# Fourier transform over row pairs t and 448-t, and attention-times-v and Fourier products in parts per step

## The chip, the cores and the metric

The kernel runs on one core of a Trainium2 chip. The metric is the device time of one execution in microseconds (us), as the median of several runs; lower is better. The engines are TensorE (PE, matrix products, with PEld for its weight loads), VectorE (DVE), ScalarE (ACT), GpSimd (POOL) and SyncE (SP, which here only issues DMAs). Each works through its own queue of instructions in order. Products go to PSUM, in tiles of one bank, and DVE or ACT take them out; POOL works on SBUF alone.

## The reference

```
scores = scale * q @ k^T                      # (8, 12, 448, 448), head size 64
scores = einsum('bhij,hg->bgij', scores, w_pre)
attn   = softmax(scores)                      # over j, +1e-9 in the denominator
attn   = einsum('bhij,hg->bgij', attn, w_post)
x      = attn @ v                             # to (8, 448, 768)
X      = fft(fft(x, axis=1), axis=2)
u      = x + real(X)
un     = layernorm(u)
out    = u + relu(un @ w_ch1) @ w_ch2         # 768 -> 3072 -> 768
```

All data are float32, the two feed-forward weights arrive as float64.

## The kernel before

The kernel has two halves. `mix_phase` computes attention, mixing and the Fourier transform and writes u to a tensor in HBM, `u_scr`; `ffn_phase` normalizes u and runs the feed-forward part on blocks of 512 rows. The change is in the first half.

**Steps.** A step handles 5 x 12 score rows on 128 partitions, twice; three steps are a block of 56 rows, six a group of 112, 24 a batch (four groups), 192 in all. `s` counts steps, and step s works ahead: it starts the premix of step s+2. In each step PE makes the premix (L294, w_pre over the heads), DVE the negative row maximum (L301), ACT the exponential and its sum (L310). POOL adds 1e-9 to the sum (L318), DVE takes the reciprocal (L320), POOL scales the two halves of the tile (L323). Two steps later PE makes the postmix (L333, w_post) and DVE turns its result by 32 x 32 blocks into `Pv` (L344). Premix and postmix have one PSUM buffer each (`pmx`, `ppo`), everything else on PE shares four (`pms`).

**Fill work** is put between these by due times. The table at L512 gives each item a step, "tile" items stand between premix and postmix, "full" items behind the postmix, "none" items are DMAs. PE and DVE run in exactly the order in which the loop (L558) writes the instructions; ACT, POOL and SP are ordered by a scheduler. The fill items are:

- transpositions of q and k (L245) and scores q k^T (L268) into `Sb`, which SP's DMAs gather into `Kr` (L284), two steps ahead of the premix;
- `emit_av` (L350): attention times v for a group, 84 matmuls of 120 columns at once; ACT or DVE copy the result to `XT` (L381);
- `emit_x` (L387): `XT` is transposed to `X`, 112 rows by 768, and POOL folds the columns d and 768-d into an even part `xe` and an odd part `xo` (L403 to L406). The transform of a real row needs the cosine table on `xe` and the sine table on `xo` alone;
- `emit_z` (L412): the transform along the rows, one of seven column chunks at a time, from the four groups (four matmuls, L417) to `z`; frequencies 0 to 224 are computed, the others are mirrored copies;
- `emit_s2` (L429): the transform along the columns for one group, four matmuls from the even chunks and three from the odd (L437); DVE adds both to `X` (L445, L448), SP stores `X` to `u_scr` (L452);
- on DVE, four operations per step of the conversion of the weights from float64 (L472 to L483); in the steps listed in `sums` one.

A batch's `emit_z` and `emit_s2` come after its 24 steps, and so fall beside the next batch's steps; those of the last batch come after the last step. `ev.pick` hands copies out of PSUM to ACT or DVE by a running count of their costs; nearly all go to ACT.

## Time and profile before

| what | before |
|---|---|
| median of 3 runs | 2830.31 us (2822.34 to 2838.7) |
| profiled execution | 2837.51 us |
| its span, first to last instruction | 2835.6 us |
| busy: PE, DVE, ACT, POOL | 91%, 44%, 26%, 23% |
| first row maximum (L301) to the last | 42.5 to 1177.2 us |
| first product of the feed-forward half (L746) | 1242.35 us |

How to read it: the shares of busy time are averages over two very different halves. From about 1242 us on PE works nearly without a break; up to there it does not, and the work is spread over four engines. Where the prediction quotes windows, a row gives a stretch in us from the span's start, its length, and for each engine the busy time and in brackets the instructions, then the granted clock of PE, the share of the DMA engines and the rate in GB/s. A row of a group gives line, engine, operation, output <- input, shapes and count, then busy time, the mean of one in ns, and the idle time ahead of it with what ended it.

### The profile page before, as it was taken

Reading aid. Unit: us, or ns where it says so; the run is one execution under the profiler, and the core shown is the slowest. Engines: PE = TensorE matmul, PEld = TensorE weight load, DVE = VectorE, ACT = ScalarE, POOL = GpSimd, SP = SyncE. Lnnn points to the kernel's source line nnn. Section 1 sums busy time; section 2 is a strip of 40 time slices with the busy share of each in tenths; the row PEclk is TensorE's granted clock in tenths of the full one; section 3 lists DMA queues with packets and bytes.
Section 4 is the critical chain, followed back from the end, with each engine's and each line's share of the span. In section 5 each row is a group of like instructions: output and inputs, shape, how many; then the busy total and the mean of one; then the engine's idle time right before and its main releaser. Section 6 shows DMA issues by size and latency. Waiting matters only on the chain.

```text
span 2835.6 us, 47087 instructions
## 1 busy us (share of the span) xinstructions
...
## 2 busy tenths in 40 slices
...
GB/s 206 175 187 131 184 131 193 131 179 134 184 130 181 134 164 135 256 299 176 156 161 156 161 158 154 167 150 168 164 147 174 141 165 183 134 161 156 156 103 106
DMA packets 185110, 463.00 MB, mean 163 GB/s; under 512 B 22990, under 2 KB 128974, under 8 KB 172350
## 3 DMA queue, kind: packets, MB, share of 16 engines
...
HBM read 317.56 MB, written 59.77 MB: 133 GB/s over the span
## 4 chain that ended last, share of the span: by engine, by line
PE 61%; issue 12%; DVE 11%; DMA 9%; ACT 3%; POOL 2%; SPq 1%; ACTq 0%; POOLq 0%; DVEq 0%
PE psP L746 10%; PE psP L786 10%; PE psR L786 7%; PE psR L746 6%; PE ms L437 5%; PE ms L361 4%; PE mx L294 4%; PE psQ L786 3%; DVE nmx L301 3%; PE ms L268 3%; PE po L333 3%; DMA w1t<-w1f 3%; PE ms L417 3%; PE psQ L746 2%; DVE Pv L344 2%
## 5 line engine op out<-in xcount | busy, mean ns | idle before, releaser
L746 PE MATMUL psP<-ub,w1t 128*128 128x256 f32 x2016 | 473.0, 388 | 24.7 <-DVE mv L705 16.6
L746 PEld LDWEIGHTS psP<-ub,w1t 128*128 128x128 f32 x2016 | 388.7, 194 | 93.4 <-DMA w1t<-w1f 20.2
L786 PE MATMUL psP<-w2t,h 128*128 128x384 f32 x1344 | 436.9, 486 | 0.0
L786 PEld LDWEIGHTS psP<-w2t,h 128*128 128x128 f32 x1344 | 254.4, 190 | 173.4
L294 PE MATMUL mx<-Kr,kw 60*64 60x448 f32 x1536 | 203.6, 584 | 143.8 <-ACT PP L310 137.6
L310 ACT ACTIVATE PP<-mx,nmx 128x448 f32<-128x448 f32 x384 | 240.2, 630 | 359.4 <-DVE nmx L301 348.0
L323 POOL TENSOR_SCALAR PP<-PP,rcp 128x448 f32<-128x448 f32 x384 | 252.6, 667 | 218.8 <-DVE rcp L320 151.6
L723 POOL TENSOR_TENSOR ub<-ub 128x768 f32<-128x768 f32 x28 | 51.0, 1842 | 1060.9 <-ACT ub L718 1060.3
L344 DVE STREAM_TRANSPOSE Pv<-po 128x896 f32<-128x896 f32 x192 | 212.9, 1109 | 148.6 <-PE po L333 147.7
L301 DVE TENSOR_REDUCE nmx<-mx 128x2 f32<-128x896 f32 x192 | 207.1, 1079 | 104.3 <-PE mx L294 102.4
L746 PE MATMUL psR<-ub,w1t 128*128 128x256 f32 x1008 | 231.7, 379 | 0.0
L786 PE MATMUL psR<-w2t,h 128*128 128x384 f32 x672 | 220.0, 486 | 0.0
L117 ACT COPY Sb<-ms 124x448 f32<-124x448 f32 x379 | 186.1, 541 | 96.5 <-PE ms L268 80.6
L746 PEld LDWEIGHTS psR<-ub,w1t 128*128 128x128 f32 x1008 | 191.2, 190 | 26.9 <-DMA w1t<-w1s 0.9
L333 PE MATMUL po<-PP,kw 60*32 60x448 f32 x3072 | 199.5, 573 | 7.5 <-DVE rcp L320 4.4
L268 PE MATMUL ms<-kT,qT 64*64 64x448 f32 (+1 forms) x1536 | 205.5, 575 | 0.0
L294 PEld LDWEIGHTS mx<-Kr,kw 60*64 60x64 f32 x1536 | 42.9, 134 | 247.8 <-ACT PP L310 198.9
L795 DVE TENSOR_TENSOR u<-u,psP 128x384 f32<-128x384 f32 x56 | 31.1, 555 | 341.6 <-PE psP L786 341.6
L786 PEld LDWEIGHTS psR<-w2t,h 128*128 128x128 f32 x672 | 126.3, 190 | 84.3
L361 PEld LDWEIGHTS ms<-Pv,vv 64*64 64x64 f32 x5376 | 154.6, 138 | 23.5 <-issue 18.4
L361 PE MATMUL ms<-Pv,vv 64*64 64x120 f32 x5376 | 158.1, 272 | 8.0 <-issue 6.2
L718 ACT COPY ub<-psQ 128x384 f32<-128x384 f32 x56 | 24.9, 481 | 497.0 <-PE psQ L716 497.0
...
## 6 DMA issues: line engine op xcount, KB each, us to landing
Kr<-Sb SPq DMA_DIRECT2D x768, 105.0 KB
...
raw<-in_moe_w_ch_dram POOLq DMA_DIRECT2D x96, 384.0 KB, 4.6
w1t<-w1f SPq DMA_DIRECT2D x84, 384.0 KB
...
```

The costliest lines, as they stand in the source:

```text
L117: self.nc.scalar.copy(out=out, in_=in_)
L268: nc.tensor.matmul(pss[x][64 * y:64 * y + r0 + 64 - lo, :S], st["qT", xx][64 * x:64 * x + 64, y, lo:r0 + 64], st["kT", xx][64 * x:64 * x + ...
L294: nc.tensor.matmul(mx[64 * z:64 * z + 64, x, :S], kw1[64 * x:64 * x + KR, :], Kr[64 * x:64 * x + KR, z, :], start=True, stop=True)
L301: nc.vector.tensor_reduce(nmx[:, :], steps[T]["mx"][:, :, :S], axis=AX.X, op=ALU.max, negate=True)
L310: nc.scalar.activation(PP[:, x, :], steps[T]["mx"][:, x, :S], ACTF.Exp, bias=steps[T]["nmx"][:, x:x + 1], accum_out=den[:, x:x + 1])
L323: nc.gpsimd.tensor_scalar(PP[:, x, :], PP[:, x, :], rcp[:, x:x + 1], 1.0, op0=ALU.mult, op1=ALU.mult)
L333: nc.tensor.matmul(po[o:o + 32, z, :S], kw2[64 * z:64 * z + KR, y, :], PP[64 * z:64 * z + KR, :, c * HS:(c + 1) * HS], start=True, stop=True)
L344: nc.vector.transpose(g["Pv"][:, T % GT, :].rearrange("p (z s) -> p z s", z=2), steps[T]["po"][:, :, :S])
L361: nc.tensor.matmul(pss[y][64 * x:64 * x + 64, pr * nu * R:(pr + 1) * nu * R], st["v"][64 * y:64 * y + 64, i, jb * D:(jb + 1) * D], _ap(Pv, ...
L437: nc.tensor.matmul(ps[:GR, :DH + 1], st["z", par, ch][:, i0:i0 + GR], tab[:w, ch, :], start=(ch == 0), stop=(ch == len(chunks) - 1))
L746: nc.tensor.matmul(p, w[m][:, i, kc, :], ub[:, i, kc, :], start=opens and kc == 0, stop=kc == NK - 1, skip_group_check=True)
L786: nc.tensor.matmul(p, lhs[i][:, half * NQ + kf, x * P:(x + 1) * P], w[:, kf, :], start=opens and half == 0 and kf == 0, stop=half == 1 and ...
```

## The change

Rows t and 448-t of a batch are treated as a pair. The cosine of the row transform is the same for both and the sine the opposite, so their sum and difference carry all that is needed: the row transform runs over 225 rows and not 448, and its result serves both rows of a pair in the column transform.

- The four groups of a batch now hold rows 0 to 111, 448 down to 337 (the first is a row of zeros), 112 to 224, and 336 down to 225 (with a row of zeros behind). The second and fourth are written to `XT` in reverse (`back`).
- Groups 0 and 1 are pair 0, groups 2 and 3 pair 1. POOL first makes sum `xs` and difference `xd` of a pair, 768 columns wide, and then the even part from the sum and the odd one from the difference. There is one fold for a pair, not for a group.
- `emit_z` has two matmuls a chunk and not four, and leaves out the mirrored copy. `emit_s2` works on a pair and one of the two parts, so a batch has four calls, with 4, 3, 4 and 3 matmuls; each is added to both groups of the pair, with the sign that the part wants. `X` has six buffers for five.
- The forward group of a pair is stored by SP. The reversed one is scattered row by row to `u_scr` by an indirect DMA of POOL; the row of zeros goes to a spare row at the end.
- `emit_av` does one of three parts a step, in three steps one behind the other. New due times go with it, and the load of v comes 1.5 steps later.

```diff
+ROWS = ((0, NB), (S - GR + 1, S - NB + 1), (GR, GR + NB), (GR * 2 + 1, GR * 2 + 1 + NB))
+PR = (GR, GR + 1)
+XW = GR + 12
...
-    def emit_av(g):
+    def emit_av(g, pr):
...
+        for jb in range(C7):
+            for x in range(2):
+                for y in range(2):
+                    i = 2 * pr + x
+                    nc.tensor.matmul(
+                        pss[y][64 * x:64 * x + 64, :nu * R],
+                        st["v"][64 * y:64 * y + 64, i, jb * D:(jb + 1) * D],
+                        _ap(Pv, 64 * y * rp + 32 * jb + R * i,
+                            [[rp, 64], [HS, nu], [1, R]]),
+                        start=(jb == 0), stop=(jb == C7 - 1))
+        if pr == 0:
+            g["XT"] = pxt.tile([P, 6, XW], F32, name="XT", tag="XT")
+        XT = g["XT"]
         rx = _row(XT)
+        back = g["gi"] % 2
...
+                o = MG + (GR - 1 - NB * e if back else NB * e)
+                sg = -1 if back else 1
+                dst = _ap(XT, (3 * y + pr) * XW + o, [[rx, P], [sg * RS, R], [sg, RS]])
+                src = _ap(pss[y], 60 * e, [[rs, P], [1, R], [R, RS]])
...
-        def fold():
-            xe = pxf.tile([GR, DH + 1], F32, name="xe", tag="xe")
-            xo = pxf.tile([GR, DH - 1], F32, name="xo", tag="xo")
-            nc.gpsimd.tensor_copy(out=xe[:, 0:DH + 1:DH], in_=X[:, 0:DH + 1:DH])
-            nc.gpsimd.tensor_tensor(xe[:, 1:DH], X[:, 1:DH], X[:, DM - 1:DH:-1],
-                                    op=ALU.add)
-            nc.gpsimd.tensor_tensor(xo[:, :], X[:, 1:DH], X[:, DM - 1:DH:-1],
-                                    op=ALU.subtract)
-            g["xf"] = (xe, xo)
-        return evs + [fold]
...
+        if g["gi"] % 2:
+            evs.append(lambda: fold(g))
+        return evs
+
+    def fold(g):
+
+        pair = g["gi"] // 2
+        n = PR[pair]
+        Xa, Xb = groups[g["b"] * NG + g["gi"] - 1]["X"], g["X"]
+        xs = pxs.tile([GR + 1, DM], F32, name="xs", tag="xs")
+        xd = pxs.tile([GR + 1, DM], F32, name="xd", tag="xd")
+        nc.gpsimd.tensor_tensor(xs[:n, :], Xa[:n, :], Xb[:n, :], op=ALU.add)
+        nc.gpsimd.tensor_tensor(xd[:n, :], Xa[:n, :], Xb[:n, :], op=ALU.subtract)
+        xe = pxf.tile([GR + 1, DH + 1], F32, name="xe", tag="xe")
+        xo = pxf.tile([GR + 1, DH - 1], F32, name="xo", tag="xo")
+        nc.gpsimd.tensor_copy(out=xe[:n, 0:DH + 1:DH], in_=xs[:n, 0:DH + 1:DH])
+        nc.gpsimd.tensor_tensor(xe[:n, 1:DH], xs[:n, 1:DH], xs[:n, DM - 1:DH:-1],
+                                op=ALU.add)
+        nc.gpsimd.tensor_tensor(xo[:n, :], xd[:n, 1:DH], xd[:n, DM - 1:DH:-1],
+                                op=ALU.subtract)
+        batches[g["b"]]["xf", pair] = (xe, xo)
...
-        for gi in range(NG):
+        for pair, n in enumerate(PR):
             nc.tensor.matmul(ps[:w, :SH + 1],
-                             groups[b * NG + gi]["xf"][par][:, d0:d0 + w],
-                             ts[:, gi, par, :],
-                             start=(gi == 0), stop=(gi == NG - 1))
-        z = pzz.tile([w, S], F32, name=f"z{par}{ch}", tag=f"z{par}{ch}")
+                             batches[b]["xf", pair][par][:n, d0:d0 + w],
+                             ts[:n, pair, par, :], start=(pair == 0), stop=(pair == 1))
+        z = pzz.tile([w, SH + 1], F32, name=f"z{par}{ch}", tag=f"z{par}{ch}")
         batches[b]["z", par, ch] = z
+        return [lambda: ev.copy(z[:, :], ps[:w, :SH + 1], SH + 1)]
...
+    def emit_s2(b, pair, par):
+
+        st = batches[b]
+        n, i0 = PR[pair], pair * GR
+        chunks, tab = ((EVEN, tce), (ODD, tdo))[par]
+        ps = ms_tile()
+        for ch, (_, w) in enumerate(chunks):
+            nc.tensor.matmul(ps[:n, :DH + 1], st["z", par, ch][:, i0:i0 + n],
+                             tab[:w, ch, :],
...
+            for back in range(2):
+                X = groups[b * NG + 2 * pair + back]["X"]
+                m = GR if back else n
+                sub, add = (ALU.subtract, ALU.add) if par else (ALU.add, ALU.add)
+                if back:
+                    sub, add = add, sub
+                nc.vector.tensor_tensor(X[:m, 0:DH + 1], X[:m, 0:DH + 1],
+                                        ps[:m, 0:DH + 1], op=sub)
+                nc.vector.tensor_tensor(X[:m, DH + 1:DM], X[:m, DH + 1:DM],
+                                        ps[:m, DH - 1:0:-1], op=add)
             ev.d += 4 * (150.0 + DH * 1.042)
-            u0 = g["b"] * S + i0
-            nc.sync.dma_start(out=u_scr[u0:u0 + GR, :], in_=X[:, :])
+            if par == 0:
+                return
+            for back in range(2):
+                X = groups[b * NG + 2 * pair + back].pop("X")
+                if back:
+                    nc.gpsimd.indirect_dma_start(
+                        out=u_scr[:, :],
+                        out_offset=bass.IndirectOffsetOnAxis(
+                            ap=rows[:GR, 2 * b + pair:2 * b + pair + 1], axis=0),
+                        in_=X[:GR, :], in_offset=None)
+                    continue
+                u0 = b * S + i0
+                nc.sync.dma_start(out=u_scr[u0:u0 + GR, :], in_=X[:GR, :])
+                if n > GR:
+                    nc.sync.dma_start(out=u_scr[u0 + GR:u0 + n, :], in_=X[GR:n, :])
...
-        for xx, (aq, ak) in enumerate(((-13, -12), (-9, -8), (-8, -7))):
+        for xx, (aq, ak) in enumerate(((-19, -19), (-8, -7), (-7, -6))):
             due("none", f + aq - 8, lambda b=b, xx=xx: emit_load_qk(b, xx))
             due("full", f + aq, lambda b=b, xx=xx: emit_xpose(b, xx, "q"))
             due("full", f + ak, lambda b=b, xx=xx: emit_xpose(b, xx, "k"))
-        due("none", f + 2, lambda b=b: emit_load_v(b))
+        due("none", f + 3.5, lambda b=b: emit_load_v(b))
         for n in range(2 * NG):
             for xx in range(3):
                 due("tile", f + BS * n - 7 + xx,
                     lambda n=2 * NG * b + n, xx=xx: emit_qk(n, xx))
         for n in range(NG):
             g = groups[b * NG + n]
-            due("tile", f + GT * n + GT + 1, lambda g=g: emit_av(g))
-            due("full", f + GT * n + GT + 2, lambda g=g: emit_x(g))
-            due("full", f + GS + 8 + n, lambda g=g: emit_s2(g))
+            for pr in range(3):
+                due("tile", f + GT * n + GT + 1 + pr, lambda g=g, pr=pr: emit_av(g, pr))
+            due("full", f + GT * n + GT + 4, lambda g=g: emit_x(g))
+        f += GS
         zs = [(0, ch) for ch in range(len(EVEN))] + [(1, ch) for ch in range(len(ODD))]
-        for x, (par, ch) in enumerate(zs):
-            due("full", f + GS + 4 + x // 2,
-                lambda b=b, par=par, ch=ch: emit_z(b, par, ch))
+        for at, (par, ch) in zip((6, 6, 7, 8, 10, 11, 11), zs):
+            due("full", f + at, lambda b=b, par=par, ch=ch: emit_z(b, par, ch))
+        for at, pair, par in ((12, 0, 0), (18, 0, 1), (23, 1, 0), (24, 1, 1)):
+            due("full", f + at, lambda b=b, pair=pair, par=par: emit_s2(b, pair, par))
+            sums.add(f + at)
...
-            ops = 0 if s < -4 else 1 if s in sums else 4
+            ops = 0 if s < -4 else 1 if s - 1 in sums else 4
```

**The order on PE.** The first rows are PE's from before, from slot 7 of a batch (the seventh step of its 24, counted from 0, here with a whole block of attention times v) to the beginning of slot 8; `ms` is a PSUM tile, `mx` the premix, `po` the postmix.

```order
L294 MATMUL mx<-Kr,kw_131 64x448 x4
L268 MATMUL ms<-kT,qT 64x448 x2
L268 MATMUL ms<-kT,qT 60x448 x2
L361 MATMUL ms<-Pv,vv 64x120 x84
L333 MATMUL po<-PP,kw_132 32x448 x8
L417 MATMUL ms<-ts,xo 127x225 x4
L294 MATMUL mx<-Kr,kw_131 64x448 x4
L268 MATMUL ms<-kT,qT 64x448 x2
L268 MATMUL ms<-kT,qT 60x448 x2
L333 MATMUL po<-PP,kw_132 32x448 x8
L437 MATMUL ms<-tce,z_5787 112x385
```

The same place in the changed kernel, slots 7 and 8 (the premix of slot 7 is the first row; L307, L281, L374, L346, L448 are the former L294, L268, L361, L333, L417):

```order
L307 MATMUL mx<-Kr,kw_134 64x448 x4
L281 MATMUL ms<-kT,qT 64x448 x2
L281 MATMUL ms<-kT,qT 60x448 x2
L374 MATMUL ms<-Pv,vv 64x120 x28
L346 MATMUL po<-PP,kw_135 32x448 x8
L448 MATMUL ms<-ts,xe 96x225 x2
L307 MATMUL mx<-Kr,kw_134 64x448 x4
L281 MATMUL ms<-kT,qT 64x448 x2
L281 MATMUL ms<-kT,qT 60x448 x2
L374 MATMUL ms<-Pv,vv 64x120 x28
L346 MATMUL po<-PP,kw_135 32x448 x8
L448 MATMUL ms<-ts,xe 96x225 x2
```

The 84 matmuls are 28 a step, the first Fourier product has two matmuls a chunk, and the second one (L437 before, seven matmuls a group in four steps running) has moved to slots 12, 18, 23 and 0.

**The order on POOL, at a fold.** Before, a fold (L403, L406, L404) stands between the addition to the sum of the exponentials (L318, `den`) and the next:

```order
L318 TENSOR_SCALAR den<-den 128x2
L403 COPY xe<-X 112x2
L406 TENSOR_TENSOR xo<-X 112x383
L404 TENSOR_TENSOR xe<-X 112x383
L323 TENSOR_SCALAR PP<-PP,rcp 128x448 x2
L318 TENSOR_SCALAR den<-den 128x2
L458 DMA raw_5459<-in_moe_w_ch_dram 128x768
L323 TENSOR_SCALAR PP<-PP,rcp 128x448 x2
```

In the changed kernel, the fold of pair 0 in slots 16 and 17 (L331 is the former L318, L336 the scaling, L227 the loads of q and k):

```order
L331 TENSOR_SCALAR den<-den 128x2
L431 TENSOR_TENSOR xs<-X 112x768
L227 DMA rawk<-in_k_dram 64x7x64 x4
L336 TENSOR_SCALAR PP<-PP,rcp 128x448 x2
L432 TENSOR_TENSOR xd<-X 112x768
L435 COPY xe<-xs 112x2
L331 TENSOR_SCALAR den<-den 128x2
L227 DMA rawq<-in_q_dram 64x7x64
L436 TENSOR_TENSOR xe<-xs 112x383
L438 TENSOR_TENSOR xo<-xd 112x383
L336 TENSOR_SCALAR PP<-PP,rcp 128x448 x2
```

The two wide operations stand in front of the next `den`, and the four loads of k between them, since the transpositions that free their buffer come in the same step.

**The order on POOL and SP, at a scatter,** with the semaphores that the rows wait for. POOL, from the middle of slot 18 on (L483 is the scatter, its output named with the size of all of `u_scr`):

```order
L227 DMA rawk<-in_k_dram 64x7x64 [waits DMASW4_49,PE_49]
L483 DMA u_scr<-X,rows 3592x768 [waits DMAHW3_49,DMASW5_49,DVE_49]
L331 TENSOR_SCALAR den<-den 128x2 [waits Activation_49]
L227 DMA rawk<-in_k_dram 64x7x64 [waits DMASW6_49]
L227 DMA rawk<-in_k_dram 64x7x64 [waits DMASW7_49]
L227 DMA rawk<-in_k_dram 64x7x64 [waits DMASW0_49]
L227 DMA rawq<-in_q_dram 64x7x64 [waits DMASW1_49,PE_49]
L336 TENSOR_SCALAR PP<-PP,rcp 128x448 [waits DVE_49]
L336 TENSOR_SCALAR PP<-PP,rcp 128x448
```

And SP's store of the other half of this pair (L490) between the gathers (L297):

```order
L297 DMA Kr<-Sb 60x1x448 [waits DMAHW2_49]
L490 DMA u_scr<-X 112x768 [waits DMAHW3_49,DMASW0_49,DVE_49]
L297 DMA Kr<-Sb 60x1x448 [waits DMAHW4_49,Activation_49]
L297 DMA Kr<-Sb 60x1x448 [waits DMAHW5_49]
L297 DMA Kr<-Sb 60x1x448 [waits DMAHW6_49]
```

The scatter waits for DVE, which makes the last addition, and for DMAHW3, the semaphore under which SP's store runs; behind it in POOL's queue stand the `den` of the next step and seven loads.

96 lines of the change are left out of this document (35 added, 61 removed).

## The prediction

> **What bounds the kernel now.** A step is the work on one tile of row mixes. Slot n is step n of a batch's 24, counted modulo 24; a batch's Fourier work falls into the slots of the next batch. Steps are counted by the row maximum (L301), one a step. First the windows of its instructions alone: batch 0, which has no Fourier work beside it, then batches 1 to 6.
>
> ```profile
> span 2835.6 us, 47087 instructions
> ...
> core 0: us, DVE busy (x), PEclk, DMA share, GB/s
> 42.54:162.57 120.03, 25.90 (x24) 0.92 0.67 190
> 162.57:1034.46 871.89, 155.27 (x144) 0.98 0.54 158
> ```
>
> Batch 0 takes 120.0 us, a later batch 871.89 / 6 = 145.3: the Fourier work costs 25.3 of them. Next the windows of all engines: four light steps (slots 22 to 1), the eight steps with the Fourier products (slots 4 to 11), and the stretch after the last step.
>
> ```profile
> core 0: us, PE busy (x) PEld busy (x) DVE busy (x) ACT busy (x) POOL busy (x), PEclk, DMA share, GB/s
> 300.04:316.80 16.76, 10.59 (x134) 3.28 (x133) 16.52 (x30) 9.23 (x25) 10.70 (x18) 1.00 0.55 180
> 340.16:399.52 59.36, 57.08 (x544) 30.48 (x543) 34.50 (x63) 24.60 (x69) 18.35 (x34) 0.99 0.37 117
> 1182.85:1242.35 59.50, 41.55 (x301) 29.03 (x302) 38.64 (x89) 7.70 (x24) 6.97 (x11) 0.86 0.94 329
> ```
>
> A light step takes 16.76 / 4 = 4.19 us. DVE is busy for 16.52 of the 16.76, PE for 2.65 a step: DVE sets it. A Fourier step takes 7.42, with PE busy for 57.08 of 59.36 and DVE 58%: PE sets it. The two bounds alternate and neither uses the other's idle time. So a us of PE work taken out of a Fourier step is worth a us, and one put into a light step is free up to 4.19 - 2.65 = 1.54. The chain of waits shows how an attention-times-v block (L361) sits in such a pair of steps (start, length, what):
>
> ```profile
> 316.88 1.00 DVE nmx L301
> ...
> 317.99 1.35 ACT PP L310 x4
> ...
> 319.38 0.98 PE mx L294 x8
> 320.36 4.43 PE ms L361 x153
> 324.79 0.75 PE ms L268 x8
> 325.54 1.00 PE po L333 x16
> ...
> 326.56 1.12 DVE Pv L344
> ...
> 329.07 0.11 DVE nmx L301
> ...
> 363.37 1.72 PE ms L417 x8
> ...
> 367.66 4.72 PE ms L437 x14
> ...
> 397.37 0.77 PE ms L245 x7
> ```
>
> One maximum releases the exponential, that the premix two steps on (one PSUM buffer), and behind the premix on PE stand the block, the scores and the postmix, which DVE's transpose waits for. This loop, from maximum to maximum over two steps, is 329.07 - 316.88 = 12.19 us.
>
> **Part 1, attention times v in thirds.** Now a block costs 12.19 - 2 x 4.19 = 3.8 over light steps; three of a batch's four stand so, the fourth (slot 7) in a PE-bound step, where it costs 4.43 - 1.54 = 2.9: 14.3 a batch. A third is 4.43 / 3 = 1.48. In the loop it gives 12.19 - 4.43 + 1.48 = 9.24 for two steps, 4.62 a step, 0.43 over the light one. Twelve thirds: 5.2. Gain 9.1 a batch, 64 for seven batches, 7.5 for batch 0 (three blocks): **71 us**. Ends: 111 if the thirds are free (1.48 is under 1.54), -26 if each costs its full 1.48; I take the loop, since it is read off the chain.
>
> **Part 2, half the Fourier products.** The eight steps cost 59.36 - 8 x 4.19 = 25.8 over light ones, 2.9 of it the block of slot 7: 22.9. Afterwards the first product (L417) has two matmuls for four, 0.86 for 1.72; the second (L437) comes as 4 and 3 matmuls, 2.70 and 2.02, two of each a batch for four of 4.72. With 2.65 beside them: slots 12 and 23 need 5.35 (+1.16 each), slot 18 with a transposition (0.77) 5.44 (+1.25), slot 0 4.67 (+0.48), slots 7 and 8 with a third 4.99 (+0.37 over part 1), slots 6 and 11 4.37 (+0.18), slot 10 nothing. Sum 5.2. The sixteen additions to X stay, four at a time, where three conversions are left out:
>
> ```profile
> L445 DVE TENSOR_TENSOR X<-X,ms 112x385 f32<-112x385 f32 x64 | 35.5, 555 | 44.5 <-PE ms L437 43.4
> L479 DVE TENSOR_SCALAR tmp<-top 128x384 uint32<-128x384 uint32 x96 | 48.8, 509 | 1.7
> ```
>
> 4 x 0.555 - 3 x 0.509 = 0.7 on DVE in four steps: 2.8. So 8.0 in place of 22.9, gain 14.9 a batch, **104 us** for seven. Ends: 160 if what is left fits into idle time, 33 if none of it does (7 x 0.86 + 2 x 4.72 = 15.5 of PE and the 2.8, so 4.6 a batch).
>
> **Part 3, GpSimd (POOL) before DVE.** Each step DVE ends with a reciprocal (L320) of a sum that POOL has first to add a constant to (L318). Whatever POOL has between two of these beyond a step's length stops DVE, and next step's maximum stands behind it. Today it hardly happens: the first row below, of the waits (us in total, times, longest).
>
> ```profile
> DVE rcp L320 <- POOL den L318: 8.6, 15, 2.7
> ...
> L323 POOL TENSOR_SCALAR PP<-PP,rcp 128x448 f32<-128x448 f32 x384 | 252.6, 667 | 218.8 <-DVE rcp L320 151.6 <-PE mx L294 41.7 <-PE po L333 19.6
> L214 POOL DMA_DIRECT2D rawk<-in_k_dram x96 | 69.3, 725 | 23.3 <-PE ms L245 18.5 <-DMA rawk<-in_k_dram 4.0
> L723 POOL TENSOR_TENSOR ub<-ub 128x768 f32<-128x768 f32 x28 | 51.0, 1842 | 1060.9 <-ACT ub L718 1060.3
> L404 POOL TENSOR_TENSOR xe<-X 112x383 f32<-112x383 f32 x32 | 34.5, 1077 | 0.0
> L406 POOL TENSOR_TENSOR xo<-X 112x383 f32<-112x383 f32 x32 | 31.7, 992 | 0.0
> L403 POOL COPY xe<-X 112x2 f32<-112x2 f32 x32 | 9.3, 291 | 34.7 <-ACT X L117 34.6
> ...
> raw<-in_moe_w_ch_dram POOLq DMA_DIRECT2D x96, 384.0 KB, 4.6
> ...
> vv<-in_v_dram POOLq DMA_DIRECT2D x16, 672.0 KB, 8.1
> u<-u_scr POOLq DMA_DIRECT2D x7, 1536.0 KB, 6.8
> ```
>
> The fold of a pair adds two operations 768 wide (1.84 each, from L723, the same shape) to 2.36 (L403, L404, L406). In the order on POOL, slot 16 has between two L318: one wide addition, four loads of k, two scalings, the other wide one, the copy: 1.84 + 2.90 + 1.33 + 1.84 + 0.29 = 8.2. Counted from that step's premix it starts at about 5.0 (maximum, exponential, X copied out), so the next L318 is done at 13.4, against 9.2 where DVE would want it: 4.2 late. Slot 4: two wide ones, scalings, the narrow three, one load (0.6): 8.0, 4.1 late. **The scatter** of the reversed rows adds a wait: its output is the whole of u_scr, so it stands on POOL until SP's store of the other half has landed, and all of POOL's queue behind it. A store is not in the landings; scaled from 384 KB in 4.6 us, 336 KB take 4.0. For pair 0 the scatter stands ahead of the next L318: additions done 3.3 after the maximum, 4.0, then 0.7 to issue (L214) and 0.3: 8.3 against 5.0, 3.3 late, and 1.0 more as seven loads crowd in behind. For pair 1 L318 goes first and only the next is late: 0.5. No scatter is in the trace: its hold lies between 0 beyond the issue, if the store has landed when POOL comes to it, and the 8.1 of the largest load here, if POOL stands until it lands; I take the issue of a load, the nearest row, and keep both ends.
>
> Together 4.2 + 4.1 + 4.8 = 13.1 a batch. While DVE stands PE runs on to the next premix, which takes back what slots 6 to 8 and 18 lack on PE, about 3: 10 a batch, 70, and 4 for batch 0's one fold: **-74 us**. Ends: 0 and -74 - 14 x 7.4 = -178.
>
> In the Trainium skill, "DMA: Bandwidth & Descriptors", section "Anatomy of one DMA — SWDGE (gpsimd) path", a transfer takes about 2.0 us plus its bytes over 436 GB/s, and the wait for a semaphore is held on the issuing sequencer. The second is this part's mechanism, and against the change. By the first the 384 KB load would take 2.9 us; the trace has 4.6, so I keep the trace; by the page the loss would be some 8 us smaller.
>
> **Part 4, small terms.** The product's PSUM tile stays taken until the additions of the next step, where block and scores want all four: 1 us a batch. DVE slows beside POOL's two-input operations:
>
> ```profile
> 299.68 0.36 DVE L479 TENSOR_SCALAR tmp<-top 128x384 uint32<-128x384 uint32 x1
> ...
> 332.53 1.55 DVE L479 TENSOR_SCALAR tmp<-top 128x384 uint32<-128x384 uint32 x1
> 332.86 0.99 POOL L406 TENSOR_TENSOR xo<-X 112x383 f32<-112x383 f32 x1
> ```
>
> The same conversion takes 1.55 for 0.36 when L406 runs. POOL's fold grows from 4 x 2.36 to 2 x 6.04, 2.6 us a batch; much of it falls where DVE waits anyway, so 1 a batch (0 to 2.6). **-14 us** for both. The Trainium skill, "GPSIMD Engine Reference", section "8. Key points", says that GpSimd shares its SBUF interfaces with VectorE and contends with some of its forms; the rows agree, and by that rule alone the full 2.6 would count, 11 us more loss.
>
> ACT copies XT in 48 small pieces for 16; four of three times the size run in 0.95 us (below), ACT is busy for 2.3 of a light step, so 3.3 of 4.6: hidden; without that cover up to 0.95 a step would be seen. The v load goes out in slot 3 and lands 8.1 later; it is wanted in slot 7, some 18 us on: hidden. SP's store waits for the additions as before, with the gathers (L284) behind it; they are issued two steps ahead of their premix, so the three or four us are hidden, and two stores and one of a single row for four make it no worse. The transpositions of q and k only move, 0.77 each into other light steps.
>
> **Part 5, after the last step.** From the end of the last postmix (1182.85) to the first product of the second half:
>
> ```profile
> 1190.83 0.95 ACT L381 COPY XT<-ms 128x180 f32<-128x180 f32 x4 [11.10 <-PE ms L361]
> 1191.08 0.84 POOL L650 DMA_DIRECT2D u<-u_scr  x1 [9.27 <-PE ms L361]
> ...
> 1209.59 1.48 DVE L703 BATCH_NORM_STATS2 st<-u 128x6 f32<-128x384 f32 x3
> ...
> 1225.13 5.47 PE L437 MATMUL ms<-tce,z 97*112 97x385 f32 x8 [11.03 <-DVE X L448]
> ...
> 1242.35 1.06 PE L746 MATMUL psP<-ub,w1t 128*128 128x256 f32 x2
> ```
>
> 59.5 us, 11.0 of it PE waiting for X. The load of u left at 1191, long before the last X. Now it stands behind the last scatter, and scatters and stores of the last batch wait for one another. PE is done some 34 us after that postmix (blocks 4.4, fold 6, halved products, a fold held by the scatter before it). The additions of pair 0 end at 33; store 4.0, scatter 4.7, store, scatter: 50; u 6.8, and 7 for statistics, transpositions and copies: 64, 5 more than now. The load took 18.5 us in this stretch (1191.08 to 1209.59) at a DMA share of 0.94, which would make it 16. I take **-8 us**.
>
> **Sum:** 71 + 104 - 74 - 14 - 8 = 79. The profiled execution took 2837.5 us (span 2835.6 and 1.9 around it), the median of the three runs is 2830.3, 0.25% lower; 2837.5 - 79 = 2758.5, set to that median 2751.
>
> **The rivals.** (a) POOL does not bind: X is out earlier than I count, and the store has landed when POOL comes to the scatter. Then part 3 is nothing to a third: gain 128 to 153, 2677 to 2702. For it: POOL is busy 10.70 of 16.76 in light steps. Against: den and reciprocal are in order every step. Chance 0.20. (b) The forecast, 2702 to 2800, 0.55. (c) The gain goes off the path: each third costs twice 0.43 (31 for part 1), and no stop of DVE is taken back (7 x 13.1 + 4 = 96): 31 + 104 - 96 - 22 = 17, 2813, and from there to 2840; 0.13. (d) Slower: the scatter holds POOL until it has landed, 14 times 8.1 for 0.7, so 104 more: 2855. It decides from 79 / 14 = 5.6 us more a scatter. For it: the trace has no such instruction; against: POOL's loads in the trace leave in 0.7 (L214). Chance 0.09. That matmuls aren't halved is no rival: the order shows two where four stood. The remaining 0.03 lies below 2677.
>
> **How the numbers follow.** About 0.5% (14 us) is what a measurement of this kernel can tell from no change. Faster: (a), (b), the rest and a quarter of (c), 0.81; within: most of (c), 0.10; slower: 0.09. The range, 2680 to 2830, leaves out (d), the upper end of (c) and the far end of (a).
>
> **What would show it.** Light steps stay at 4.2, steps with a third at 4.6 to 4.7, none at 7 to 9. L437's successor halves its count. The wait of the reciprocal for POOL grows from 8.6 us to some 60 to 90, at slots 17, 5 and 19; the scatter shows waiting for SP's store. If that wait stays small, (a) holds. If thirds show PE waiting for PSUM or ACT, (c). If POOL stands 5 us and more at the scatter itself, (d). The forecast is wrong if steps without any of these are longer than 4.2.

## The result and the profile after

The changed kernel takes **2751.3 us** (median of four runs, 2746.4 to 2761.1), the kernel before, run beside it, 2826.3 us (four runs, 2821.7 to 2838.7). The ratio is 0.9732, 95% interval 0.9688 to 0.9776: faster by 75 us. The profiled execution took 2746.39 us, its span is 2744.6, 91.0 less than that of before; it was the lowest of its four, and before's (2837.51) stood near its highest, so the profiles differ by more than the medians.

First the windows of the row maximum alone (its instruction is L314 now), for batch 0, batches 1 to 6, and batch 7 up to its last maximum (start and end, length, busy time and count, granted clock, DMA share, GB/s).

```profile
52.60:172.04 119.44, 25.78 (x25) 0.91 0.65 180
172.04:940.20 768.16, 154.61 (x144) 0.97 0.61 179
940.20:1064.85 124.65, 24.77 (x24) 0.92 0.53 171
```

A later batch takes 768.16 / 6 = 128.0 us where it took 145.3. Batch 0 hardly changes (119.4 for 120.0). The first maximum comes at 52.6 and not at 42.5: 10.1 us are lost before the first step. Next the groups by line: the products and the blocks on PE, and the wide fold on GpSimd.

```profile
L374 PE MATMUL ms<-Pv,vv 64*64 64x120 f32 x5376 | 181.0, 278 | 16.9 <-ACT Sb L128 15.4 <-issue 1.2 <-DVE X L475 0.2
L448 PE MATMUL ms<-ts,xe 113*96 113x225 f32 (+3 forms) x128 | 32.3, 386 | 10.5 <-POOL xe L436 6.8 <-ACT Sb L128 3.6
L462 PE MATMUL ms<-tce,z 96*112 96x385 f32 (+3 forms) x128 | 46.2, 503 | 0.0
L432 POOL TENSOR_TENSOR xd<-X 112x768 f32<-112x768 f32 (+1 forms) x16 | 32.1, 2004 | 0.0
```

Each Fourier product has 128 records on the even side where it had 256 (the profile shows two for a matmul); the thirds have as many as the blocks had. Of the waits, the prediction named the one of DVE's reciprocal for GpSimd's sum (us in total, times, longest):

```profile
DVE rcp L333 <- POOL den L331: 38.1, 28, 5.6
```

It had been 8.6. The timeline of one slot 17 shows the stop, and a second thing beside it (start, length, engine, line). Slot n runs here from the row maximum of step n+2, whose premix the loop's step n starts, to the next.

```profile
657.15 2.33 DVE L517 SCALAR_TENSOR_TENSOR top<-raw,top 128x384 uint32<-128x384 uint32 x1
...
660.23 2.05 DVE L521 SCALAR_TENSOR_TENSOR tmp<-raw,tmp 128x384 f32<-128x384 uint32 x1
662.66 0.17 DVE L333 RECIPROCAL rcp<-den 128x2 f32<-128x2 f32 x1 [0.38 <-POOL den L331]
...
655.52 2.86 POOL L227 DMA_DIRECT2D rawk<-in_k_dram  x4
658.42 1.55 POOL L336 TENSOR_SCALAR PP<-PP,rcp 128x448 f32<-128x448 f32 x2
659.95 1.91 POOL L432 TENSOR_TENSOR xd<-X 112x768 f32<-112x768 f32 x1
...
662.42 0.21 POOL L331 TENSOR_SCALAR den<-den 128x2 f32<-128x2 f32 x1
```

The slot is 8.3 us long (654.48 to 662.75), as forecast. But DVE hardly waits in it: two conversions that take 0.56 us elsewhere take 2.33 and 2.05, the first beside GpSimd's four loads of k and its scaling, the second beside the wide subtraction (L432). Then the stretch after the last step, on GpSimd and PE.

```profile
1090.18 1.02 POOL L483 DMA_INDIRECT u_scr<-X,rows  x1 [13.95 <-DVE w2t L723]
...
1113.25 0.97 POOL L483 DMA_INDIRECT u_scr<-X,rows  x1 [16.43 <-DVE X L475]
1124.58 0.94 POOL L483 DMA_INDIRECT u_scr<-X,rows  x1 [10.35 <-DMA w2s<-w2t]
1130.65 1.61 POOL L693 DMA_DIRECT2D u<-u_scr  x2 [5.13 <-issue]
...
1152.54 1.06 PE L789 MATMUL psP<-ub,w1t 128*128 128x256 f32 x2
```

The load of u leaves behind the third scatter, at 1130.65; the first product of the second half starts at 1152.54, 87.7 us after the last maximum (1064.85), against 1242.35 - 1177.20 = 65.2 before. Last the head, in the timelines of SP's queue and of PE.

```profile
6.78 9.49 SPq L212 DMA_DIRECT2D tce<-k_tc  x1
...
45.23 1.75 PE L307 MATMUL mx<-Kr,kw 60*64 60x448 f32 x2 [6.56 <-DMA Kr<-Sb]
```

The table behind ts needs 9.49 us to leave, and the first premix waits 6.56 for its gather. In the kernel before it was 0.41 and 4.92:

```profile
6.46 0.41 SPq L199 DMA_DIRECT2D tce<-k_tc  x1
...
39.10 2.65 PE L294 MATMUL mx<-Kr,kw 60*64 60x448 f32 x5 [4.92 <-DMA Kr<-Sb]
```

The 91.0 us of the spans are so: head -10.1, batch 0 +0.6, batches 1 to 6 +103.8 (872.0 - 768.2), batch 7 up to its last maximum +18.0 (142.6 - 124.7), from there to the second half -22.5, and the second half +1.2.

### The profile page after: what moved, and what is told of

It reads as the page before. It is cut to its first block, busy times and chain, and to the rows that moved or that the text cites. A ratio compares the mean times of both kernels' runs of the same rounds, so it can differ in the third digit from the quotient of the medians.

```text
span 2744.6 us, 46540 instructions
## 1 busy us (share of the span) xinstructions
PE 2476.4 (90%) x18544; PEld 1587.2 (58%) x18544; DVE 1262.2 (46%) x2238; ACT 724.0 (26%) x2135; POOL 732.0 (27%) x1117
## 4 chain that ended last, share of the span: by engine, by line
PE 41%; issue 9%; DMA 7%; DVE 1%; POOL 0%; SPq 0%; POOLq 0%; ACT 0%
PE psP L829 12%; PE psP L789 10%; PE psR L829 7%; PE psR L789 6%; PE psQ L829 3%; DMA w1t<-w1f 3%; PE psQ L789 2%; DMA u<-u_scr 2%; DMA out_dram<-u 2%; DMA w1t<-w1s 1%; PE psQ L759 1%; DVE st L746 0%; POOL ub L766 0%; DVE u L838 0%; SPq L703 0%
## 5 line engine op out<-in xcount | busy, mean ns | idle before, releaser
L336 POOL TENSOR_SCALAR PP<-PP,rcp 128x448 f32<-128x448 f32 x384 | 259.6, 686 | 154.0 <-DVE rcp L333 109.4
L307 PE MATMUL mx<-Kr,kw 60*64 60x448 f32 x1536 | 204.0, 589 | 97.0 <-ACT PP L323 88.2
L314 DVE TENSOR_REDUCE nmx<-mx 128x2 f32<-128x896 f32 x192 | 206.2, 1074 | 34.9 <-PE mx L307 23.9
L281 PE MATMUL ms<-kT,qT 64*64 64x448 f32 (+1 forms) x1536 | 205.3, 568 | 7.0 <-DVE X L475 6.3
L374 PEld LDWEIGHTS ms<-Pv,vv 64*64 64x64 f32 x5376 | 169.4, 142 | 67.2 <-issue 38.7
L346 PE MATMUL po<-PP,kw 60*32 60x448 f32 x3072 | 194.1, 562 | 9.1 <-DVE rcp L333 7.7
L374 PE MATMUL ms<-Pv,vv 64*64 64x120 f32 x5376 | 181.0, 278 | 16.9 <-ACT Sb L128 15.4
L307 PEld LDWEIGHTS mx<-Kr,kw 60*64 60x64 f32 x1536 | 42.2, 135 | 207.1 <-ACT PP L323 153.9
```

The lines of the kernel that those rows point to most:

```text
L281: nc.tensor.matmul(pss[x][64 * y:64 * y + r0 + 64 - lo, :S], st["qT", xx][64 * x:64 * x + 64, y, lo:r0 + 64], st["kT", xx][64 * x:64 * x + ...
L307: nc.tensor.matmul(mx[64 * z:64 * z + 64, x, :S], kw1[64 * x:64 * x + KR, :], Kr[64 * x:64 * x + KR, z, :], start=True, stop=True)
L314: nc.vector.tensor_reduce(nmx[:, :], steps[T]["mx"][:, :, :S], axis=AX.X, op=ALU.max, negate=True)
L336: nc.gpsimd.tensor_scalar(PP[:, x, :], PP[:, x, :], rcp[:, x:x + 1], 1.0, op0=ALU.mult, op1=ALU.mult)
L346: nc.tensor.matmul(po[o:o + 32, z, :S], kw2[64 * z:64 * z + KR, y, :], PP[64 * z:64 * z + KR, :, c * HS:(c + 1) * HS], start=True, stop=True)
L374: nc.tensor.matmul(pss[y][64 * x:64 * x + 64, :nu * R], st["v"][64 * y:64 * y + 64, i, jb * D:(jb + 1) * D], _ap(Pv, 64 * y * rp + 32 * jb ...
```

## The experiments

### The two halves of the change, each alone

Thirds alone, on the kernel before:

```diff
-            due("tile", f + GT * n + GT + 1, lambda g=g: emit_av(g))
-            due("full", f + GT * n + GT + 2, lambda g=g: emit_x(g))
-            due("full", f + GS + 8 + n, lambda g=g: emit_s2(g))
+            for pr in range(3):
+                due("tile", f + GT * n + GT + 1 + pr, lambda g=g, pr=pr: emit_av(g, pr))
+            due("full", f + GT * n + GT + 4, lambda g=g: emit_x(g))
+            due("full", f + GS + 10 + n, lambda g=g: emit_s2(g))
...
-        due("none", f + 2, lambda b=b: emit_load_v(b))
+        due("none", f + 3.5, lambda b=b: emit_load_v(b))
...
```

> The kernel before with attention times v dealt out in thirds and nothing else of the change: the folds, the Fourier products over four row groups, the additions and the plain stores stay (they stand two steps later, since X is complete two steps later). By part 1 of the prediction a third costs 0.43 us of a light step and a block 3.8: 71 us faster than before, about 2755 against 2826. The rival, read from the changed kernel's steps (those with a third take 5.2 to 5.5 us there, not 4.62, so about 1.0 more than a light step): 12 us a batch against the 14.3 of the blocks, so only 20 us faster, about 2806. If thirds are free below the 1.54 us of idle PE in a light step: 111 us, 2715.

The row pairs alone, the changed kernel with the block put back:

```diff
-            for pr in range(3):
-                due("tile", f + GT * n + GT + 1 + pr, lambda g=g, pr=pr: emit_av(g, pr))
+            due("tile", f + GT * n + GT + 1, lambda g=g: emit_av(g))
...
```

> The changed kernel with the attention times v put back as one block in the first of its three steps; fold over row pairs, halved products and scatter stay. By the prediction's sum 71 us are lost again: 2822 against 2751, about as slow as the kernel before (parts 2 to 5 alone come to 8 us). If thirds are worth only 20 us: 2771, and the folded transform is worth the other 55. If, with the Fourier steps now light, a block costs its full 3.8 us in all four places of a batch, 14.3 + 0.9 against 5.2: 2824.

Measured: thirds alone **2849.3 us against 2829.7, 0.7% slower** (ratio 1.0074, 1.0051 to 1.0096); row pairs alone 2817.4 against the same 2829.7 (0.9951, 0.9933 to 0.9969). All three expectations for the thirds missed; 2822 for the pairs held. The windows of the maximum show where: for each kernel batches 1 to 6, and the eleven slots 4 to 14 of the fifth batch. Thirds alone:

```profile
165.99:1040.27 874.28, 155.31 (x144) 0.96 0.53 158
...
630.65:716.24 85.59, 11.94 (x11) 0.94 0.45 136
```

Row pairs alone:

```profile
172.87:1005.90 833.03, 154.94 (x144) 0.94 0.55 165
...
623.90:689.41 65.51, 11.86 (x12) 0.92 0.43 140
```

Before, and then the changed kernel:

```profile
631.45:705.87 74.42, 11.93 (x11) 1.00 0.44 138
```

```profile
586.38:645.88 59.50, 11.81 (x12) 0.97 0.61 180
```

| kernel | a batch | slots 4 to 14 | the other thirteen |
|---|---|---|---|
| before | 145.3 | 75.8 | 69.5 |
| thirds alone | 145.7 | 84.6 | 61.1 |
| row pairs alone | 138.8 | 62.0 | 76.8 |
| both | 128.0 | 59.7 | 68.3 |

(All columns are means over batches 1 to 6; the rows above with 11 or 12 instructions are the fifth batch alone.) Thirds alone gain 8.4 a batch in the thirteen slots and lose 8.8 in the eleven. That a third adds its matmuls to a step that PE fills already is at most a part of this loss. Slots 5 and 6 alone take 5.0 more (16.6 for 11.6): the load of v leaves 1.5 steps later in this kernel, its second half lands 12 to 13 us after issue (8 to 10 before), PE waits in slot 5 for gathers, and in slot 6 it works without a break at a lower granted clock (0.63 in the fifth batch). That the load holds up the gathers is read from the trace; the last run below, with v in pieces, fits it. The two slots in the fifth batch:

```profile
634.74:644.12 9.38, 5.09 (x35) 1.30 (x32) 4.89 (x10) 2.31 (x6) 4.85 (x9) 0.81 0.89 217
644.12:653.30 9.18, 9.18 (x46) 4.50 (x48) 4.10 (x7) 3.47 (x10) 2.50 (x5) 0.63 0.56 182
```

The second product, two steps later in that kernel, now stands in slots 10 to 13: slots 12 to 14 take 10.1 more, slots 4 and 7 to 11 take 6.3 less.

Behind the row pairs the thirds gain in both groups, 8.5 and 2.3. The largest piece is again not the block's own step: slot 3 takes 10.2 on the mean with the block and 4.2 with thirds. PE stands there for gathers, in the fifth batch for 5.2 us:

```profile
621.67 1.45 PE L307 MATMUL mx<-Kr,kw 60*64 60x448 f32 x3 [5.19 <-DMA Kr<-Sb]
```

Nine gathers leave there one behind the other from 607.98 on, with the load of v beside them at 608.43. Slots 3 to 5 give 6.7 of the 10.8 a batch, the other eleven steps that hold a block or a third 2.9. Whether the block makes these gathers late, since it stands ahead of the scores, was not tried.

So, by the ratios to the kernel before of the same session, the thirds are worth (0.9951 - 0.9732) x 2830 = 62 us behind the row pairs (66 by the medians), and less than nothing without them. The gain of 75 is neither half's; it comes from the two together.

### What stops DVE while GpSimd folds

Three runs, each on the changed kernel: GpSimd's addition ahead of the reciprocal left out; the conversions taken out of the slots in which the fold runs; and both.

```diff
-        nc.gpsimd.tensor_scalar(den[:, :], den[:, :], 1e-9, None, op0=ALU.add)
```

> The changed kernel without GpSimd's addition of the constant to the sum ahead of DVE's reciprocal (the constant, 1e-9, is left out; the sum is at least 1, so it rounds away). DVE's reciprocal then waits for ACT alone, and what POOL is late goes into the scaling, which has two steps until its postmix. Theory (POOL in front of DVE stops it, part 3): the 38 us that the reciprocal waits for POOL go, and slots 5 and 17 fall from 8.4 towards 4.5 to 6: 35 to 65 us faster than the changed kernel, 2686 to 2716. Rival 1 (the stop is DVE slowed by GpSimd's wide operations beside it, 32 us over all conversions, not the order): the wait goes but steps stay above 7: under 20 us. Rival 2 (the postmix waits instead): slots 5 and 17 shrink and the slots two later grow by as much: within 10 us of 2751.

```diff
             ops = 0 if s < -4 else 1 if s - 1 in sums else 4
+            if s >= 0:
+                ops = {5: 0, 17: 0, 18: 0, 2: 6, 7: 6, 8: 6, 9: 6, 14: 6, 20: 6}.get(s % GS, ops)
```

> The changed kernel with the weight conversions taken out of the steps in which GpSimd folds (slots 5, 17 and 18: none) and dealt to slots 2, 7, 8, 9, 14 and 20 (six instead of four), where PE sets the step. Without the addition to the sum the steps 5 and 17 had stayed at 7.5 to 9.8 us: DVE's conversions L516 to L522, 0.36 to 0.56 each elsewhere, took 2.0 to 2.3 beside the fold. Theory (two stops of the same size stand side by side, the order on POOL and DVE held by GpSimd's wide operations; taking one away leaves the other): here the reciprocal still waits for POOL's sum, so slot 17 stays near 8 and the wait of the reciprocal grows from 38 to some 55 to 70 us; slot 18 loses its 1.6 (L523 at 2.15 for 0.51): 5 to 20 us faster than the changed kernel, 2731 to 2746. Rival (the hold beside the fold alone is the stop): 45 us faster, 2706.

> Both stops taken away: conversions moved out of slots 5, 17 and 18, and no addition by GpSimd ahead of the reciprocal (the constant 1e-9 is left out). Theory (two stops side by side): now slot 17 falls from 8.3 to 4.5 to 5.5 and slot 18 from 7.2 to about 5.5, slot 5 only in part, because the gathers (L297) stand behind the load of v there: 25 to 45 us faster than the changed kernel, 2706 to 2726. Rival 1 (a third limit as long, the order on ACT or the scaling before the postmix): under 10 us. Rival 2 (the conversions cost in the steps that take them what they save): under 10 us, and slots 7 to 9, 14 and 20 longer by 1 us each.

Measured: 2748.5, 2760.0 and 2752.7 us; ratios to before 0.9711 (0.9675 to 0.9746), 0.9736 (0.971 to 0.9762) and 0.972 (0.9698 to 0.9742), where the changed kernel has 0.9732 (0.9688 to 0.9776). None can be told from it: the gains expected of all three did not come. The windows of slots 5, 17 and 18 of the fifth batch say more: first the row of slot 17 (length; busy time of PE, its weight loads, DVE, ACT, GpSimd), then the sum of the three slots. The changed kernel:

```profile
654.48:662.75 8.27, 7.70 (x76) 3.38 (x69) 7.55 (x8) 5.59 (x12) 8.08 (x11) 1.00 0.66 208
...
sum 23.89, PE 20.10 PEld 10.94 DVE 20.16 ACT 13.36 POOL 23.34; mean PE 6.70 PEld 3.65 DVE 6.72 ACT 4.45 POOL 7.78
```

Without the addition:

```profile
664.74:672.24 7.50, 6.93 (x73) 2.98 (x66) 7.16 (x7) 5.58 (x12) 7.47 (x10) 1.00 0.69 214
...
sum 24.05, PE 17.96 PEld 9.10 DVE 19.61 ACT 13.45 POOL 23.93; mean PE 5.99 PEld 3.03 DVE 6.54 ACT 4.48 POOL 7.98
```

With the conversions moved:

```profile
667.60:675.28 7.68, 7.11 (x74) 3.09 (x67) 2.29 (x3) 5.58 (x12) 7.49 (x11) 1.00 0.62 189
...
sum 22.22, PE 16.98 PEld 8.43 DVE 8.59 ACT 13.31 POOL 21.68; mean PE 5.66 PEld 2.81 DVE 2.86 ACT 4.44 POOL 7.23
```

With both:

```profile
658.42:663.46 5.04, 4.47 (x50) 2.17 (x46) 2.25 (x3) 4.67 (x12) 5.01 (x7) 1.00 0.57 173
...
sum 15.97, PE 12.22 PEld 6.11 DVE 8.62 ACT 12.71 POOL 15.94; mean PE 4.07 PEld 2.04 DVE 2.88 ACT 4.24 POOL 5.31
```

Leaving out the addition alone leaves the three slots where they were, moving the conversions alone takes 1.7 us out of them, and both take 7.9 (means over batches 1 to 6: 24.2 in the changed kernel, then 24.5, 22.7 and 18.3). Without the addition DVE is busy for 7.16 of 7.50 us, its conversions drawn out. With the conversions gone it is busy for 2.29 of 7.68 and waits for GpSimd's sum; over that whole run:

```profile
DVE rcp L333 <- POOL den L331: 100.8, 30, 5.6
```

So **two stops of about one size stand side by side**, and whoever takes away one meets the other. The third run's expectations for the slots held (on the mean 5.0 and 5.6 in slots 17 and 18, 7.7 in slot 5). The first run's missed (9.8 and 7.5 in slots 5 and 17), and in the second the wait went past the 55 to 70 us expected. What the slots lost did not reach the end. A batch takes 128.6 (771.72 us for six in the windows). Slots 2, 14 and 20, which got two conversions more, grew by 1.1 to 1.5 each (mean over batches 1 to 6), slot 4 by 1.6 and slot 22 by 1.0; for the last two I have no cause.

### The additions in other slots

```diff
-        for at, pair, par in ((12, 0, 0), (18, 0, 1), (23, 1, 0), (24, 1, 1)):
+        for at, pair, par in ((10, 0, 0), (22, 0, 1), (23, 1, 0), (24, 1, 1)):
```

> The changed kernel with the second Fourier product at slots 10, 22, 23 and 0 in place of 12, 18, 23 and 0, so that only one of its four sets of additions, not three, falls into a step in which a third wants PSUM tiles. Theory (the tile held until the additions, part 4, costs more than the 1 us a batch of the prediction: 2.3 at slot 13 alone, where the third waits 2.2 us): slot 13 from 7.3 to about 5.4, slots 18 and 19 together from 12.4 to about 9.5, slots 10, 22 and 23 up by 1 to 2 together: 3 a batch, 15 to 25 us faster than the changed kernel, 2726 to 2736. Rival (the additions and products cost the same in any step): within 7 us of 2751.

Measured: 2754.7 us, 0.9729 (0.9704 to 0.9754): no difference. Slot 13 fell from 7.3 to 4.9 and slot 18 from 7.2 to 5.3, but slot 23 rose from 4.4 to 7.9, slot 10 from 4.0 to 5.9 and slot 19 from 5.2 to 6.5 (means over batches 1 to 6). The product and its additions cost about as much where they go; what the PSUM tile held alone costs isn't told apart by this.

### The scatter and the end

A plain store in the scatter's place, and then the scatter kept, with the rows of u in tensors of their own:

```diff
                 if back:
-                    nc.gpsimd.indirect_dma_start(
...
+                    p0 = 1 - pair
+                    r0 = b * S + S - GR * (pair + 1) + 1
+                    nc.sync.dma_start(out=u_scr[r0:r0 + GR - p0, :], in_=X[p0:GR, :])
                     continue
```

> The changed kernel with the indirect scatter replaced by a plain store from SP of the same rows, in the order of X (the reversal of the rows is left out). No wait of POOL for SP's store, and the load of u for the second half can leave early. By the prediction's terms: scatter 4.8 us a batch, 34, and 8 in the tail: 42 us faster than the changed kernel, 2709. By what its trace shows (the scatter waits 2.3 us and issues in 1.0, slot 19 is only 0.6 over a third's step; the stretch after the last step is 22 us longer): 5 to 15 in the steps and 15 in the tail: 20 to 30 us faster, 2720 to 2731. Rival (the tail is long for the products and folds, not for the scatter): under 10 us faster.

```diff
-    u_scr = scr.tile([B * S + B, DM], F32, name="u_scr")
+    u_scr = {(b, x): scr.tile([n, DM], F32, name=f"u_scr{b}{x}")
+             for b in range(B) for x, n in enumerate((2 * GR + 1, GR, GR))}
...
-                        out=u_scr[:, :],
+                        out=u_scr[b, 2 - pair][:, :],
```

> The changed kernel with the rows of u in tensors of their own, for each batch one for the stored rows and one for each of the two scatters, so that a scatter waits for its X alone and the load of u for its own rows alone; the scatter itself stays on GpSimd, and a load of u becomes four to seven pieces. Theory (the end is longer by 22 us because the load of u stands behind the last stores and scatters, which wait for one another): from the last maximum to the first product of the second half 64 to 72 us in place of 87.7, and 0 to 1 a batch in the steps (scatter without its wait of 2.3 us): 15 to 28 us faster, 2723 to 2736. Rival 1 (the pieces of the load cost GpSimd's queue in the second half what the end gains): within 5 us of 2751. Rival 2 (the scatter's hold, the prediction's 4.8 us a batch, is real): up to 50 us faster, 2700.

Measured: the plain store 2745.5 us (0.9713, 0.968 to 0.9746), the split scratch **2709.3 us (0.9567, 0.9546 to 0.9589)**. With the plain store the second half begins 63.9 us after the last maximum (1086.34), so 24 of the 87.7 are gone, where 15 were expected; but they are given back in the steps: a batch takes 131.9 for 128.0. The total is within the rival's 10 us, but not for its reason. Slot 21 is 8.2 us long for 4.3, since PE waits for a gather there, and the four loads of k just ahead of it land 10.1 to 11.1 us after issue (in the fifth batch of the changed kernel 4.2 to 5.1):

```profile
696.13 1.72 PE L307 MATMUL mx<-Kr,kw 60*64 60x448 f32 x2 [3.04 <-DMA Kr<-Sb]
...
1150.26 1.06 PE L787 MATMUL psP<-ub,w1t 128*128 128x256 f32 x2
```

Whether the second store does it by its place on SP's queue, ahead of gathers, or because GpSimd, free of the scatter, sends the loads earlier, isn't told apart. With the split scratch nothing is given back: the load of u starts at 1075.66, ahead of the last two scatters, and the second half begins 61.0 us after the last maximum (1050.29).

```profile
1075.66 1.23 POOL L698 DMA_DIRECT2D u<-u_scr  x2 [2.54 <-PE ms L373]
...
1103.96 1.02 POOL L482 DMA_INDIRECT u_scr<-X,rows  x1 [2.88 <-DVE X L474]
1107.66 1.01 POOL L482 DMA_INDIRECT u_scr<-X,rows  x1 [2.68 <-DVE X L474]
1111.29 1.06 PE L794 MATMUL psP<-ub,w1t 128*128 128x256 f32 x2
```

Of its span of 2700.0, 44.6 less than the changed kernel's, 26.7 come from this stretch, 14.6 from ahead of it (1064.85 - 1050.29: batches 1 to 6 take 126.9 each for 128.0, batches 0 and 7 3.4 and 4.5 less), and 3.4 from the second half. So the scatter's wait costs about 1 us a batch (slot 19 falls from 5.2 to 4.0), as the theory had it and not rival 2, and the dependence on one tensor 27 at the end, where 16 to 24 were expected.

### The head

The first batch's loads at their old due times, on the split scratch:

```diff
-        for xx, (aq, ak) in enumerate(((-19, -19), (-8, -7), (-7, -6))):
-            due("none", f + aq - 8, lambda b=b, xx=xx: emit_load_qk(b, xx))
+        at = ((-19, -19), (-8, -7), (-7, -6)) if b else ((-13, -12), (-9, -8), (-8, -7))
+        for xx, (aq, ak) in enumerate(at):
+            due("none", max(f + aq - 8, 1) if b else aq - 8,
+                lambda b=b, xx=xx: emit_load_qk(b, xx))
```

> The split scratch, and beside it the first batch's loads and transpositions of q and k at the due times of the kernel before, and no load of q and k for the second batch due ahead of step 1. Theory (the first maximum comes at 52.6 us and not at 42.5 because the loads of the second batch's first pair of heads run beside the first gathers; the prediction had no term for it): first maximum at 42 to 45 us, the rest as in split_scratch: 2709 - 8 = 2701. Rival (the head is longer because the three pairs are transposed in another order and the tables' load holds the queue for 9.5 us): first maximum stays at 50 or above, 2709.

Measured: 2706.7 us (0.9576, 0.9541 to 0.961), first maximum at 52.77: the theory fell, the order of the loads is not it. What was left was the load of ts, which has 113 rows since the change. It was cut into 112 rows and 1:

```diff
-        for t, n in ((rows, "at"), (ts, "ts"), (tce, "tc"), (tdo, "td")):
+        nc.sync.dma_start(out=rows, in_=cn["at"].ap())
+        for a, z in ((0, GR), (GR, GR + 1)):
+            nc.sync.dma_start(out=ts[a:z], in_=cn["ts"].ap()[a:z])
+        for t, n in ((tce, "tc"), (tdo, "td")):
             nc.sync.dma_start(out=t, in_=cn[n].ap())
```

> The split scratch, and the load of the cosine and sine table ts (now 113 rows, 112 before the change) cut into 112 rows and 1 row. Theory (the load of 113 rows does not spread over the DMA engines as one of 112 did: in the changed kernel the next table's load takes 9.5 us to leave, not 0.4, and the first gathers land 9 to 14 us after they leave, not 6, while the engines are busy 10 to 50%): the tables leave in 0.3 to 0.5 each and the first maximum comes at 42 to 46 us in place of 52.8: 2709 - 8 = 2701. Rival (the hold is the fourth table or the prefetch of the second batch): first maximum stays at 50 or above.

Measured: **2694.8 us (0.9507, 0.9486 to 0.9527)**, first maximum at 40.59, 12.2 earlier than in the split scratch (52.79). The next table leaves in 0.35 us, and the first premix waits 3.63 for its gather:

```profile
7.25 0.35 SPq L214 DMA_DIRECT2D tce<-k_tc  x1
...
34.55 1.71 PE L309 MATMUL mx<-Kr,kw 60*64 60x448 f32 x2 [3.63 <-DMA Kr<-Sb]
```

### A version that beats both

Two more runs took the fold off GpSimd. In the first it runs on DVE, one step later, without the addition; in the second ts is cut as well, and v lies in three tiles of two heads a side, each loaded when its third is done. Both have one conversion for four in slots 5 and 17, and five in slots 7, 8 and 9.

```diff
-        nc.gpsimd.tensor_tensor(xs[:n, :], Xa[:n, :], Xb[:n, :], op=ALU.add)
-        nc.gpsimd.tensor_tensor(xd[:n, :], Xa[:n, :], Xb[:n, :], op=ALU.subtract)
+        nc.vector.tensor_tensor(xs[:n, :], Xa[:n, :], Xb[:n, :], op=ALU.add)
+        nc.vector.tensor_tensor(xd[:n, :], Xa[:n, :], Xb[:n, :], op=ALU.subtract)
...
-        due("none", f + 3.5, lambda b=b: emit_load_v(b))
+        for pr in range(3):
+            due("none", f + 1.5 + pr, lambda b=b, pr=pr: emit_load_v(b, pr))
```

> As split_head, and the five operations of a fold moved from GpSimd to DVE, one step later, with three conversions of that step dealt to slots 7, 8 and 9; GpSimd's addition of 1e-9 to the sum is left out. Theory (GpSimd's fold stops DVE for some 4 us a fold, by the order before the reciprocal and by holding DVE's conversions, and both are gone when DVE folds itself in about 3 us, 2 x 0.95 + 2 x 0.5 + 0.1): slots 5, 17 and 18 fall from 8.8, 8.3 and 7.2 to about 6, 6 and 5.5, less 1 to 2 a batch for the conversions moved: 5 a batch, 30 us faster than split_head, 2671. Rival (what is taken out of the fold's steps comes back in others, as with the conversions moved): within 10 us of split_head.

> The split scratch, ts in two pieces, the fold on DVE without GpSimd's addition of 1e-9 (as in split_head_fold_dve, where slot 17 fell from 8.3 to 6.4 but slot 5 stayed at 9.6, since ACT's copy of the scores waits there for gathers that stand behind the load of v), and v in three tiles of two heads a side, each loaded when the third that reads it is done, so that the load spreads over slots 1 to 4. Theory (slot 5 is held third by the gathers behind v's load): slot 5 falls from 9.6 to 6 to 7, about 3 a batch, 20 us, and 8 at the head: about 2675. Rival (the DMA time is only moved to slots 1 to 4, or the pieces hold the gathers of those steps): slot 5 falls and slots 1 to 4 grow by as much: 2692.

Measured: 2701.9 us (0.9569, 0.9531 to 0.9607), no faster than split_head: slots 17 and 18 fell to 6.4 and 5.5, but slot 5 went to 9.6, since ACT's copy of the scores waits there for DMAs behind the load of v. In the run without the addition the same copy waited for a gather:

```profile
605.42 0.97 ACT L128 COPY Sb<-ms 124x448 f32<-124x448 f32 x2 [2.62 <-DMA Kr<-Sb]
```

With v spread out it is **2657.7 us (0.9368, 0.9344 to 0.9392)**, 177 us under the kernel before, where 2675 was expected. Slot 5 falls too, from 9.6 to 6.5, and slots 1 to 4 do not grow for it (the cut of ts acts at the head alone). Batches 1 to 6, and slots 5 and 17 of the fifth batch:

```profile
156.85:895.64 738.79, 155.25 (x144) 0.98 0.63 184
```

```profile
557.34:563.70 6.36, 5.54 (x58) 2.51 (x62) 6.33 (x11) 4.92 (x11) 5.24 (x8) 1.00 0.76 239
618.38:624.71 6.33, 5.38 (x66) 2.35 (x62) 6.30 (x12) 6.04 (x13) 6.18 (x8) 1.00 0.66 178
```

A batch takes 123.1 for the 126.6 of split_ts112, and the stretch after the last maximum 55.2 (1016.98 to 1072.15) for 64.6. With the fold on DVE and v in one piece a batch took 126.0 (756.14 / 6), so most of this comes with v in pieces. The price of the other edits apart wasn't tried.

## Why the prediction came out right

The time was forecast to the microsecond (2751), and that is partly luck: terms that were off cancelled. By the spans, batches 1 to 7 gained 121.8 us (103.8 + 18.0) where 84 were forecast (7 x 12.0), and the head, batch 0 and the end came out 27.5 worse (10.1, 2.9 and 14.5). By the medians the gain is 75 for the 79 forecast; the kernel before, run again, stood 4 us lower too.

- **The two bounds** (DVE sets a light step, PE a Fourier step) agree in sign: the same thirds gain in the one kind of step and lose in the other. Much of the size lies elsewhere, in gathers and in PE's granted clock. (The window of light steps that the prediction calls slots 22 to 1 is slots 20 to 23 as the loop counts; no block stands in them, so the 4.19 holds.)
- **Part 1, 71 us:** some 62 measured, behind the row pairs, but not by the prediction's way. Its two prices were both too low. A step with a third takes 5.3 on the mean of the twelve, so 1.1 over a light step and not 0.43, nearer to rival (c); but a block had cost more than the 3.8 read off one loop, since the steps behind it were long too (slots 1 to 4 take 24.5 in before, 16.8 if light). Behind the row pairs, 6.7 of the 10.8 a batch lie in slots 3 to 5, with the gathers, and 2.9 in the other steps with a block or a third, where the prediction had 9.1. It did not say that the 71 exist only once part 2 has shortened the products.
- **Part 2, 104 us:** not measured by itself, since the fold comes with it; with the row pairs alone, slots 4 to 14 fall by 13.8 a batch.
- **Parts 2 to 5, together 8:** 12 measured (0.49%, 0.31 to 0.67). In the batches they gave more than forecast, at both ends less. A batch was forecast to gain 12.0 and gained 17.3.
- **Part 3, the fold (4.2 and 4.1 late):** the size is right, slots 5 and 17 stand at 8.8 and 8.3, and 7.9 went out of the three slots in the fifth batch (5.9 on the mean) when both stops were gone. The mechanism is half of it. The order on GpSimd is one of two stops; part 4 held the other, DVE slowed beside GpSimd, for a term of 1 us a batch to be added, while it fills the same time. That is why the reciprocal's wait is 38 us and not 60 to 90; with the conversions moved away it is 100.8. What the fold costs the whole kernel was not shown: with both stops gone it took 2752.7.
- **Part 3, the scatter (4.8 a batch):** mis-sized, about 1. The store that it waits for was estimated at 4.0 us; the scatter of a slot 1 waited 2.32, and took 1.03 to issue, not 0.7:

```profile
576.22 1.03 POOL L483 DMA_INDIRECT u_scr<-X,rows  x1 [2.32 <-DMA u_scr<-X]
```

- **Part 4, the PSUM tile (1 a batch):** not settled.
- **Part 5, the end (-8):** mis-sized, -22.5. The chain scatter, store, scatter, load was seen, and priced 14 too short; 26.7 us of that stretch go with tensors of their own.
- **The head (no term):** -10.1. The tables' loads stood nowhere in the prediction; ts shrank from 787 to 397 KB, but went from 112 rows to 113.
- **Batch 0** gained 0.6, not 3.5.
- **The rivals:** (a) fell as a forecast (2677 to 2702), and slots 5 and 17 are as long as GpSimd's fold makes them, though taking that away alone did not shorten the whole. (c) was nearly right on the thirds and wrong on the whole. (d) fell: the scatter's instruction takes 1.0 us, and slot 19, where it stands, 5.2.
- **The signs:** two failed. Slot 13, with a third, takes 7.3 us, where none was to stand at 7 to 9; PE waits 2.2 there for a copy by ACT. Slot 18 takes 7.2 for the 5.44 of part 2; DVE is busy for 7.17 of its 7.24 us in the fifth batch, 2.15 of them with one conversion beside the fold.
